# Eight small products in a row in front of a slot, in a kernel of attention and two layers

## The chip, the cores and the metric

The kernel runs on one core of a Trainium2 chip. The metric is the device time of one execution in microseconds, the median of several runs. TensorE (PE in the profile) multiplies, VectorE (DVE), ScalarE (ACT) and GpSimd (POOL) work on elements, and SyncE (SP) issues the DMAs.

## What is computed

Nystrom attention (4 batches, 8 heads, 576 tokens, head size 64, 32 landmarks), then two feed-forward layers of 2304 tokens, 512 wide, 2048 inside:

```python
q_lm = q.reshape(B, H, m, S // m, D).mean(axis=3)      # m = 32 landmarks
k_lm = k.reshape(B, H, m, S // m, D).mean(axis=3)
A, Bm, C = sm(q, k_lm), sm(q_lm, k_lm), sm(q_lm, k)    # softmaxes
Z = Bm.transpose(0, 1, 3, 2) / (norms of Bm)
for _ in range(6):
    Z = 2 * Z - Z @ Bm @ Z
x = A @ Z @ C @ v                                      # then heads side by side
h = x @ w_in;  x = (h * clip(h + 3, 0, 6) / 6) @ w_out
h = x @ w_in2; out = where(h > 0, h, exp(min(h, 0)) - 1) @ w_out2
```

## The kernel before

The attention is never multiplied out. For each batch a Newton stage (`newton`: landmarks, softmaxes, the inverse in six steps, and `finish`) makes a small matrix `mt` from Z, C and v. N = `mt` times the first layer's input weights takes the place of those weights, so that the first layer's h is A times N. N is made in four **parts** of 512 columns (`attn_n(b, c)`, line 764): for each of four 32-row blocks j and two head groups g one **product**, 64 deep, 32 wide, 512 columns, so eight products in a part. They write two PSUM banks of the pool "bk", which has two. ScalarE then copies each bank to `nh`, and VectorE subtracts to get the rest `nl` (a number is kept as a high and a low half). The input weights of a part come by DMA into the tile `w1c`, of which there are two, so that the part c + 2 can be loaded (`load_w1`, four DMAs on SP) when the part c has read its own.

The main work runs in **slots** (loop at line 1117). A batch has 32 slots: two halves of its tokens by 16 blocks of 128 inner units. `slot_a1` (line 791) makes h with six matmuls from `nh`, `nl` and the attention halves `ath`, `atl`; then ScalarE (relu into `gf`), VectorE, ScalarE (`gh`) and GpSimd (`gl`) make the activation. `slot_a2` (line 821), three slots later, adds the block to four outputs x with twelve matmuls from `gh`, `gl` and the weights. The h tile has two buffers. Part c of N is read by slots 4c to 4c + 3 of the first half, and again in the second half.

Beside the slots the planner places the Newton stage of the next batch, the parts of N (before: in slots 20, 24 and 28 of the batch before, and in slot 0 for the last part), and every third slot a conversion of later weights (`conv_out2`, `conv_in2`: a load, work on ScalarE, VectorE and GpSimd, a store).

The order on each engine is fixed when the program is built. Each step gets a due time (`wanted`, in slots), and a planner with its own model of durations puts the instructions of each engine in order. Two things bind it: data dependencies, and orders written by hand with `after` (line 117), which only say that one instruction is to be planned behind another. On one engine such an order costs no wait. All matmuls of the attention, `amm`, hang in one chain (`last`); the matmuls of the slots are free against them. `marks["slot"]` is the last matmul of the newest `slot_a1`.

Of the kernel before, what the change touches and what calls it, by code (L numbers as in the profile page):

```python
# [31 lines left out]
def nystrom_ffn_kernel(ctx: ExitStack, tc, q, k, v, w_in1, w_out1, w_in2, w_out2, out):  # L32
# [32 lines left out]
    B, G, _, _, S = q.shape  # L65
# [9 lines left out]
    NKT = DFF // 128  # L75
# [8 lines left out]
    MPC = W // 128  # L84
# [10 lines left out]
    GATE1, O2, NEW1 = 8, 3, 0  # L95
    PACE, NEW, PACE1 = 0.5, -4, 0.2
    XSET, XPACE = 4, 1

    strict = [False]

# [16 lines left out]
    def after(inst, other):  # L117

        tc.add_manual_dep(
            inst.ins, other.name, mybir.DependencyInfo(mybir.DependencyClass.NoSync, mybir.DependencyReason.DATA)  # L120
        )
# [4 lines left out]
    def sub(o, a, b, eng=vec):  # L126
        return eng.tensor_tensor(out=o, in0=a, in1=b, op=ALU.subtract)
# [18 lines left out]
    def mm(o, w, x, start, stop):  # L146
        return pe.matmul(o, lhsT=w, rhs=x, start=start, stop=stop)

    def wanted(s):
        tc.cur_priority = int(1000 * (s + 100))  # L150

    last = [None]

    def ordered(inst):

        if last[0] is not None:
            after(inst, last[0])
        last[0] = inst.ins
# [7 lines left out]
    def amm(*a):  # L166
        ordered(mm(*a))

    def atr(*a):
        ordered(pe.transpose(*a))  # L170

    x1d = dram.tile([NDM, 128, NT], F32, name="x1d")
    w1d = dram.tile([NDM, 128, DFF], F32, name="w1d")
# [5 lines left out]
    banks, marks = {}, {}  # L179

    def bank():
        return banks["att"].tile([128, 512], F32, name="bk", tag="bk")
# [48 lines left out]
    def run(gen):  # L231
        for _ in gen:
            pass
# [176 lines left out]
    def load_w1(b, c):  # L410
        t = w1_t[b, c] = w1_tile()
        for i in range(MPC):
            o = c * W + i * 128
            sp.dma_start(out=t[:, i], in_=w1d[:, :, o:o + 128].rearrange("k p n -> p k n"))
# [277 lines left out]
    def start():  # L692
# [15 lines left out]
        def fill(eng):  # L708
# [7 lines left out]

        make = {
            "k": preps, "f": lambda: finish(0, kept["Q"], cvs, sc), "n": lambda: attn_n(0, 0, 128),
            "i": lambda: keep("Q", inverse(EB, sb)), "t": lambda: attn_at(0, 0, vec),
        }  # L720
# [25 lines left out]
    def span(b, hf):  # L746

        n = T1 if b == 0 else HALF
        return (0, n) if hf == 0 else (n, S - n)

    def attn_at(b, hf, eng=pool):

        s, n = span(b, hf)
        ath = nat.tile([128, G, n], F32R, name="ath", tag=f"ath{hf}")
        atl = nat.tile([128, G, n], F32R, name="atl", tag=f"atl{hf}")
        for g in range(G):
            at = ft.tile([128, T2], F32, name="at", tag="at" if g or b or hf else "gf", bufs=1 if g or b or hf else 2)[:, 0:n]
            vec.transpose(out=at, in_=e_t[b, g][:, s // 32:(s + n) // 32, :].rearrange("p t l -> p (t l)"))
            yield
            act.copy(out=ath[:, g, :], in_=at)  # L760
            sub(atl[:, g, :], at, ath[:, g, :].bitcast(F32), eng)
        at_t[b, hf] = (ath, atl)

    def attn_n(b, c, n=W):

        nh = nat.tile([128, G, W], F32R, name=f"nh{c}", tag=f"nh{c}")
        nl = nat.tile([128, G, W], F32R, name=f"nl{c}", tag=f"nl{c}")
        n_t[b, c] = (nh, nl)
        w1 = w1_t[b, c]
        mt = mt_t[b]  # L770
        for o in range(0, W, n):

            nps = [bank()[:, 0:n] for _ in range(G)]
            for j in range(4):
                for g in range(G):
                    p0 = 64 * g
                    amm(nps[g][32 * j:32 * j + 32, :], mt[p0:p0 + 64, j, :],
                        w1[p0:p0 + 64, o // 128:(o + n) // 128, j, :], True, True)
            for g in range(G):
                h, l = nh[:, g, o:o + n], nl[:, g, o:o + n]  # L780
                act.copy(out=h, in_=nps[g])
                sub(l, nps[g], h.bitcast(F32))
            yield
        nb, nc_ = (b, c + 2) if c + 2 < NW else (b + 1, c + 2 - NW)
        if 0 < nb < B:
            load_w1(nb, nc_)
# [4 lines left out]
    def slot_a1(i):  # L791
        b, hf, m = i // SB, i // NKT % 2, i % NKT
        nt = span(b, hf)[1]
        ps = banks["h"].tile([128, 512], F32, name="h", tag="h")[:, 0:nt]
        c, o = m // MPC, m % MPC * 128
        nh, nl = n_t[b, c]
        ath, atl = at_t[b, hf]
        n = 0
        for g in range(G):
            for w, x in ((nh, atl), (nl, ath), (nh, ath)):  # L800
                marks["slot"] = mm(ps, w[:, g, o:o + 128], x[:, g, :], n == 0, n == 3 * G - 1).ins
                n += 1
        gf = ft.tile([128, T2], F32, name="gf", tag="gf", bufs=2)[:, 0:nt]
        yield
        act.activation(out=gf, in_=ps, func=AF.Relu, scale=1.0 / 6.0, bias=half_b)
        yield
        if i < NKT:
            g = gp.tile([128, T2], F32, name="g", tag="gh")[:, 0:nt]
            vec.scalar_tensor_tensor(out=g, in0=gf, scalar=1.0, in1=ps, op0=ALU.min, op1=ALU.mult)
            gt[i] = g, None  # L810
            return
        gh = gp.tile([128, T2], F32R, name="gh", tag="gh")[:, 0:nt]
        gl = gp.tile([128, T2], F32R, name="gl", tag="gl")[:, 0:nt]
        vec.scalar_tensor_tensor(out=gf, in0=gf, scalar=1.0, in1=ps, op0=ALU.min, op1=ALU.mult)
        yield
        act.copy(out=gh, in_=gf)
        yield
        sub(gl, gf, gh.bitcast(F32), vec if i >= NA - SB + XSET else pool)
        gt[i] = (gh, gl)

    def slot_a2(i, mm=mm):
        b, hf, kk = i // SB, i // NKT % 2, i % NKT
        gh, gl = gt.pop(i)
        s, nt = span(b, hf)
        for dm in range(NDM):
            if kk == 0:
                acc[dm] = banks["x"].tile([128, 512], F32, name="x", tag="x")[:, 0:nt]
            sl = slice(dm * 128, (dm + 1) * 128)
            if i < NKT:
                mm(acc[dm], wo[kk][:, sl], gh, kk == 0, kk == NKT - 1)  # L830
            else:
                wh, wl = wo[kk]
                for j, (w, x) in enumerate(((wh, gh), (wh, gl), (wl, gh))):
                    mm(acc[dm], w[:, sl], x, kk == 0 and j == 0, kk == NKT - 1 and j == 2)
            if kk == NKT - 1:
                t0 = b * S + s
                xs = ft.tile([128, nt], F32, name="xs", tag="xs", bufs=NDM)
                act.copy(out=xs, in_=acc[dm])
                sp.dma_start(out=x1d[dm, :, t0:t0 + nt], in_=xs)
            yield  # L840
# [205 lines left out]
    def second_half(slots):  # L1046
# [7 lines left out]
        def parts():  # L1054
            for c in range(NW):
                yield from attn_n(1, c, 256)
# [60 lines left out]
    for i in range(END, NA):  # L1117
        b, r = i // SB, i % SB

        wanted(i)  # L1120
        if r == 0:
            run(attn_n(b, NW - 1))
            run(attn_at(b, 1))
            if b + 1 < B:
                newton(b + 1)
            else:
                att.close()
                win.append(ctx.enter_context(tc.tile_pool(name="win", bufs=1, side="right", reuse_waits="tile")))
                xp.append(win[0])
                x0 = load_x(0, vec)  # L1130
        if b + 1 < B and r == NKT:
            run(attn_at(b + 1, 0))
        if b + 1 < B and r > NKT and r % MPC == 0:
            run(attn_n(b + 1, (r - NKT) // MPC - 1))
        if (i - END) % O2 == 0 and conv:
            gate[0] = marks["slot"]
            wanted(i + 4)
            conv.pop(0)()
            gate[0] = None
        if i >= NA - SB + XSET:  # L1140
            wanted(i + 4)
            next(x0, None)
        if i == NA - 14:
            wanted(i + 2)
            load_in2(0)
        wanted(i)
        run(slot_a1(i))
        run(slot_a2(i - DELAY))

    def late():  # L1150

        for i in range(NA - DELAY, NA):
            a2 = slot_a2(i, bmm)
            for _ in range(NDM):
                next(a2)
                yield
            run(a2)

    def seconds():
        for q in range(NTT * NQ):  # L1160
            yield from second(q)
# [3 lines left out]
    behind, tail, xs, n = seconds(), late(), x0, 0  # L1165
# [59 lines left out]
```

## Time and profile before

| | |
|---|---|
| median of 3 runs | 870.97 us (870.86 to 872.89) |
| the profiled execution | 872.62 us |
| its span | 870.8 us |
| granted clock, mean | 0.976 of 2.4 GHz |
| PE busy | 824.6 us (95%) |
| DVE, ACT, POOL busy | 519.2, 450.9, 321.9 us |

The time of the profiled execution is its span and 1.8 us around it. Matmuls overlap, so PE is counted busy from the first start to the last end; a busy PE may still do little. One product of fp32 numbers shows as two records. All engine instructions go through one helper, so every row names line 109, and instructions are told apart by their tiles: h and x are the slots' matmuls, bk those of the attention, "bk<-w1c,mt" the products of N.

### The profile page before, as it was taken

The numbers are of one execution on the slowest core, as the hardware profiler recorded it, in microseconds if no ns is written. First come the engines' busy times: TensorE is split into PE (matmuls) and PEld (weight loads), VectorE is DVE, ScalarE is ACT, GpSimd is POOL, SyncE is SP. The second block draws the span as 40 slices with busy tenths as digits, with TensorE's granted clock in tenths as the row PEclk, the third lists the DMA queues.
The fourth block names the chain that finished last, engine by engine and source line by source line (L and its number), as shares of the span: only waits on it lengthen the run. The fifth ranks groups of instructions, "written<-read, shape, count | busy, mean of one in ns | idle before, by whom it ended". The sixth has DMA issues, their size and how long they took to land.

```text
span 870.8 us, 15636 instructions
## 1 busy us (share of the span) xinstructions
PE 824.6 (95%) x5746; PEld 704.2 (81%) x5746; DVE 519.2 (60%) x1054; ACT 450.9 (52%) x1008; POOL 321.9 (37%) x330
## 2 busy tenths in 40 slices
PE   4778899999999999999999799999999999999998
PEld 3656678778985789858989699998989889999996
DVE  5579857647542465326688787775566554654544
ACT  2368645555553556537566565655454443443433
POOL 2257656636543445432244794551083000000000
PEclk9759999999999999999999899999999999999999
DMA  9377942285454532535366647677846556565441
GB/s 323 119 266 244 347 147 75 87 259 191 148 156 148 159 120 102 160 108 181 126 240 246 197 174 276 249 269 260 285 167 209 180 174 234 197 217 182 163 152 73
DMA packets 95564, 165.65 MB, mean 190 GB/s; under 512 B 7232, under 2 KB 51264, under 8 KB 95488
## 3 DMA queue, kind: packets, MB, share of 16 engines
q1 hardware_dynamic: 95488, 164.66, 55.8%
q8 instruction: 45, 0.74, 0.4%
q14 instruction: 31, 0.25, 0.1%
HBM read 119.54 MB, written 45.09 MB: 189 GB/s over the span
## 4 chain that ended last, share of the span: by engine, by line
PE 74%; DVE 7%; DMA 5%; POOL 4%; ACT 2%; issue 2%; SPq 0%; DVEq 0%; POOLq 0%; ACTq 0%
PE x L109 39%; PE h L109 28%; PE bk L109 7%; DVE h L109 1%; DMA kt<-in_k 1%; POOL x L109 1%; DMA out<-ob 1%; POOL xf L109 1%; DMA x<-x1d 1%; DVE w1c L109 1%; DVE y L109 1%; DVE gf L109 1%; DMA u<-in_moe_w_in 1%; DMA w1c<-w1d 1%; SPq L109 0%
## 5 line engine op out<-in xcount | busy, mean ns | idle before, releaser
L109 PE MATMUL h<-x,wi 128*128 128x384 f32 x1008 | 207.7, 341 | 6.4 <-DVE u L109 2.0
L109 PE MATMUL x<-gh,wo 128*128 128x288 f32 x896 | 204.3, 301 | 0.3 <-DVE wo L109 0.3
L109 PEld LDWEIGHTS h<-x,wi 128*128 128x128 f32 x1008 | 182.8, 190 | 21.8 <-DVE u L109 3.2
L109 PEld LDWEIGHTS x<-gh,wo 128*128 128x128 f32 x896 | 150.6, 188 | 18.2 <-issue 12.9
L109 PE MATMUL x<-gl,wo 128*128 128x288 f32 x448 | 131.8, 296 | 1.3 <-DVE gl L109 1.3
L109 ACT CAST gh<-gf 128x288 fp32r<-128x288 f32 (+1 forms) x172 | 79.1, 460 | 83.0 <-DVE gf L109 82.5
L109 PE MATMUL x<-w,gh 128*128 128x512 f32 x360 | 116.2, 393 | 0.0
L109 POOL TENSOR_TENSOR gl<-gf,gh 128x288 fp32r<-128x288 f32 x84 | 69.6, 830 | 98.7 <-ACT gh L109 88.9
L109 ACT ACTIVATE gf<-y 128x384 f32<-128x384 f32 x96 | 50.4, 525 | 98.7 <-DVE y L109 98.5
L109 DVE SCALAR_TENSOR_TENSOR gf<-gf,y 128x384 f32<-128x384 f32 x96 | 64.5, 672 | 59.0 <-ACT gf L109 59.0
L109 ACT ACTIVATE gf<-h,half_b 128x288 f32<-128x288 f32 x128 | 63.7, 500 | 62.0 <-PE h L109 52.2
L109 PE MATMUL h<-atl,nh 128*128 128x288 f32 x256 | 81.6, 319 | 9.9 <-DVE g L109 8.5
L109 DVE SCALAR_TENSOR_TENSOR gf<-gf,h 128x288 f32<-128x288 f32 x112 | 50.0, 448 | 66.9 <-ACT gf L109 66.2
L109 PE MATMUL x<-w,ghl 128*128 128x512 f32 x324 | 89.1, 392 | 0.0
L109 PEld LDWEIGHTS x<-gl,wo 128*128 128x128 f32 x448 | 84.4, 188 | 2.9 <-DVE gl L109 1.9
L109 PE MATMUL h<-ath,nh 128*128 128x288 f32 x256 | 77.9, 304 | 0.0
L109 PE MATMUL h<-ath,nl 128*128 128x288 f32 x256 | 77.8, 304 | 0.0
L109 PEld LDWEIGHTS x<-w,gh 128*128 128x128 f32 x360 | 67.4, 189 | 9.1
L109 PE MATMUL x<-w,gl 128*128 128x512 f32 x180 | 70.7, 393 | 0.0
L109 DVE TENSOR_TENSOR gl<-gf,gh 128x384 fp32r<-128x384 f32 (+1 forms) x88 | 57.6, 658 | 19.6 <-ACT gh L109 15.0
L109 PEld LDWEIGHTS h<-atl,nh 128*128 128x128 f32 x256 | 49.2, 192 | 22.7 <-DVE g L109 12.7
L109 PEld LDWEIGHTS x<-w,ghl 128*128 128x128 f32 x324 | 60.2, 188 | 8.4
(147 smaller groups left out, 1304.6 us busy)
## 6 DMA issues: line engine op xcount, KB each, us to landing
wi<-wi2p SPq DMA_DIRECT2D x64, 448.0 KB, 5.0
w<-wo2p SPq DMA_DIRECT2D x32, 512.0 KB, 6.0
wi2p<-wi SPq DMA_DIRECT2D x32, 448.0 KB, 2.7
u<-in_moe_w_in SPq DMA_DIRECT2D x25, 512.0 KB, 4.5
w1c<-w1d SPq DMA_DIRECT2D x48, 256.0 KB, 4.5
ub<-in_moe_w_out SPq DMA_DIRECT2D x16, 512.0 KB, 6.2
u<-in_moe_w_out SPq DMA_DIRECT2D x16, 512.0 KB, 4.3
wo2p<-w SPq DMA_DIRECT2D x16, 512.0 KB, 3.0
```

The costliest lines, as they stand in the source:

```text
L109: inst = getattr(self.eng, name)(*a, **kw)
```

## The change

In the third and fourth batch (b of 2 and 3) the first product of a part is ordered behind the last matmul of the slot before, of `slot_a1` (`marks["slot"]`) and of `slot_a2` (`prev[0]`), and all later matmuls of slots are ordered behind the part's last product (`hold`). The function `smm` stands in the place of `mm` in the slots for that. The parts 0 to 2 move to slots 25, 28 and 31 of the batch before; part 3 stays in slot 0.

```diff
     XSET, XPACE = 4, 1
+    NAT = 25, 28, 31
...
+    hold, prev = [None], [None]
+
+    def smm(*a):
+
+        inst = mm(*a)
+        if hold[0] is not None:
+            after(inst, hold[0])
+        prev[0] = inst.ins
+        return inst
...
             for j in range(4):
                 for g in range(G):
                     p0 = 64 * g
-                    amm(nps[g][32 * j:32 * j + 32, :], mt[p0:p0 + 64, j, :],
-                        w1[p0:p0 + 64, o // 128:(o + n) // 128, j, :], True, True)
+                    inst = mm(nps[g][32 * j:32 * j + 32, :], mt[p0:p0 + 64, j, :],
+                              w1[p0:p0 + 64, o // 128:(o + n) // 128, j, :], True, True)
+                    ordered(inst)
+                    if b > 1 and g == j == 0:
+                        after(inst, marks["slot"])
+                        after(inst, prev[0])
+            if b > 1:
+                hold[0] = last[0]
...
-                marks["slot"] = mm(ps, w[:, g, o:o + 128], x[:, g, :], n == 0, n == 3 * G - 1).ins
+                marks["slot"] = smm(ps, w[:, g, o:o + 128], x[:, g, :], n == 0, n == 3 * G - 1).ins
...
-    def slot_a2(i, mm=mm):
+    def slot_a2(i, mm=smm):
...
-        if b + 1 < B and r > NKT and r % MPC == 0:
-            run(attn_n(b + 1, (r - NKT) // MPC - 1))
+        if b + 1 < B and r in NAT:
+            run(attn_n(b + 1, NAT.index(r)))
```

## Rows read from the trace of the kernel before

**Rows 1.** The page, part 1: busy us of each engine (share of the span), instructions.

```profile
PE 824.6 (95%) x5746; PEld 704.2 (81%) x5746; DVE 519.2 (60%) x1054; ACT 450.9 (52%) x1008; POOL 321.9 (37%) x330
```

**Rows 2.** Stages: us, busy us (instructions) of each engine, granted clock, DMA share, GB/s.

```profile
247.00:286.00 39.00, 39.00 (x228) 24.12 (x227) 13.03 (x26) 17.19 (x38) 15.39 (x17) 1.00 0.54 163
...
357.00:396.00 39.00, 39.00 (x219) 23.18 (x218) 11.63 (x23) 15.54 (x33) 13.66 (x15) 1.00 0.50 158
```

**Rows 3.** Chain of waits in order of time, third batch's parts: start, us, what, instructions.

```profile
247.92 1.08 PE bk L109 x16
249.00 0.59 PE x L109 x3
...
251.97 0.80 PE h L109 x6
...
254.72 1.01 PE bk L109 x14
...
261.64 0.97 PE bk L109 x2
262.62 0.33 PE h L109
...
268.15 0.98 PE bk L109 x6
...
270.91 0.80 PE h L109 x6
271.71 1.58 PE x L109 x12
```

**Rows 4.** The same chain in the stretch of the fourth batch's parts.

```profile
358.00 1.02 PE bk L109 x16
359.02 1.52 PE x L109 x10
...
364.73 1.01 PE bk L109 x14
...
394.36 0.98 PE bk L109 x4
```

**Rows 5.** Timeline of VectorE: start, us, instruction, idle before and releaser.

```profile
250.58 1.29 DVE L109 TENSOR_TENSOR nl<-bk,nh 128x512 fp32r<-128x512 f32 x2 [0.98 <-ACT nh L109]
...
257.78 1.29 DVE L109 TENSOR_TENSOR nl<-bk,nh 128x512 fp32r<-128x512 f32 x2 [0.98 <-ACT nh L109]
...
269.80 1.29 DVE L109 TENSOR_TENSOR nl<-bk,nh 128x512 fp32r<-128x512 f32 x2 [0.48 <-ACT nh L109]
```

**Rows 6.** Timeline of SP's DMA issues, and the landing times of w1c, 246 to 290.

```profile
258.06 2.81 SPq L109 DMA_DIRECT2D w1c<-w1d  x4
...
359.15 8.72 SPq L109 DMA_DIRECT2D w1c<-w1d  x8
...
DMA to landing us min/median/max: 2.8/4.5/5.5
```

**Rows 7.** Timeline of VectorE: the copies that make mt.

```profile
247.57 0.28 DVE L109 COPY mt<-bk 128x128 f32<-128x128 f32 x1
...
355.59 0.28 DVE L109 COPY mt<-bk 128x128 f32<-128x128 f32 x1
```

**Rows 8.** Waits, 190 to 400 us: who on whom, us, times, longest.

```profile
PE bk L109 <- ACT EC L109: 0.4, 1, 0.4
...
ACT y L109 <- DMA u<-in_moe_w_out: 22.0, 9, 5.6
```

**Rows 9.** The page, part 5: busy us and mean ns of one, idle before.

```profile
L109 ACT ACTIVATE gf<-h,half_b 128x288 f32<-128x288 f32 x128 | 63.7, 500 | 62.0 <-PE h L109 52.2
...
L109 DVE SCALAR_TENSOR_TENSOR gf<-gf,h 128x288 f32<-128x288 f32 x112 | 50.0, 448 | 66.9 <-ACT gf L109 66.2
```

**Rows 10.** Chain of waits, 288 to 356 us: two of the Newton stage's pieces.

```profile
308.07 1.05 PE bk L109 x52
...
340.57 0.36 PE bk L109 x16
```

## The prediction

> **What bounds the kernel now.** I read the page first: TensorE (PE) is busy for 824.6 of the 870.8 us of the span [rows 1], so the question is what PE does in the stretches that the change touches. The stage table answers that: the two stretches in which the parts of N for the third and fourth batch are made, 247 to 286 us and 357 to 396 us, have PE busy throughout at a granted clock of 1.00 (the 2.4 GHz level), while VectorE, ScalarE and GpSimd work 12 to 17 us of 39 [rows 2]. PE's own wait list from 190 to 400 us holds one wait of 0.4 us, and that one lies outside both stretches [rows 8]. So PE sets the pace, and busy doesn't mean well used: the chain of waits, in order of time, shows what it is busy with.
>
> A slot without anything beside it is six matmuls into h (0.80 us) and twelve into x (1.58 us): 18 matmuls in 2.38 us, 0.132 us each [rows 3]. A part of N is eight products, sixteen records, 64 rows deep and 32 columns wide, so eight of them sit in the array side by side. Sixteen records in a row take 1.02 to 1.08 us on the chain; a piece of two records takes 0.97 us [rows 3, 4]. A piece costs what its longest member costs, whatever stands in it. The one slot matmul behind a piece then stands at 0.33 us instead of 0.13 [rows 3]. So a piece of two costs 0.97 + 0.20 = 1.17 us, a whole part 1.02 + (1.52 - 10 x 0.132) = 1.22 us in the fourth batch and 1.08 + 0.19 = 1.27 us in the third (three slot matmuls behind it took 0.59 us for 0.40).
>
> Counted on the chain, the parts of the third batch stand in 1, 2, 6 and 6 pieces, those of the fourth in 1, 2, 6 and 7: 31 pieces for 8 parts. Rows 3 and 4 show the whole parts, the long piece of each second part, and first and last of chopped ones; the others repeat them. From the third part on the planner puts one h matmul of a slot between every two records.
>
> **What the change does to that.** The ordering edges: the first product of a part goes behind the last matmul of the slot before (`marks["slot"]`, `prev[0]`), and every later slot matmul goes behind the part's eighth product (`hold`). All of these are orders on PE's own queue, so they add no instruction and no semaphore. The chain `last` already ties the products to each other and to Newton's matmuls, so nothing is left that could come between. I take 8 rows for 31 pieces.
>
> The parts also move, from slots 20, 24 and 28 of a batch to 25, 28 and 31 (the fourth stays at slot 0 of the next). With each go two ScalarE copies, two VectorE subtractions and four w1c loads on SP, past the store and load of one or two weight conversions, which come every third slot. GpSimd gets and loses nothing.
>
> The sum by stage: 39.00 us hold 228 matmuls in the third batch's stretch, 64 of them products and two reaching in from before; 162 x 0.132 = 21.4 us, so the parts cost 17.6 us. In the fourth, 219 - 66 = 153, 20.2 us, parts 18.8 us [rows 2]. Together 36.4 us, 1.17 for each of 31 pieces, which is the price read off the chain. Eight whole rows at 1.22 to 1.27 are 9.8 to 10.2 us; I take 10.0. **Gross gain 26.4 us**, all on PE, the engine that sets the end. Whatever follows is PE's too, so it moves forward whole.
>
> What was hidden in those 36 us and isn't any longer. A row in front of a slot holds the whole slot back if one of its inputs is late; in pieces, it held back little.
>
> - *mt.* Slots are counted back from the fourth part, which is planned with slot 0. In the trace the first part ran late anyway, in front of slot 24 in one batch and within it in the other, since mt came only then: its copy ends at 247.85 and 355.87 us [rows 7]. Slot 25's first matmul stands at 251.97 and at 359.02 + 1.52 = 360.54 us [rows 3, 4]; less the part that ran before it, 250.7 and 359.3. Spare 2.8 and 3.4 us: cost 0.
> - *The banks.* A part needs both banks of its pool, so row four (slot 0 of the next batch) waits for the copies of row three, one slot before. Between them lie 2.38 + 0.2 = 2.6 us. From the end of a part to the end of the second VectorE subtraction took 250.58 + 1.29 - 249.00 = 2.9 us, 3.3 us (from 255.73) and, where ScalarE was at it at once, 271.09 - 269.13 = 2.0 us [rows 3, 5]. Late by -0.6 to +0.7 us: cost 0 to 1.4 us for two batches. I take 0.8, nearer to the two late rows, as these stood behind whole rows.
> - *w1c.* The load that row four needs starts when row two has read its tile. After the second part the four issues began 2.3 us later and took 2.8 us; the slowest landed 5.5 us after its issue: 10.6 us at worst. In the fourth batch the issues ended 2.1 us after the part; with 4.5 us in the median, 6.6 [rows 4, 6]. Between row two and row four lie four slots and row three, 9.5 + 1.2 + 0.2 = 10.9 us: cost 0, bound 2 us if the queue stands behind a store. No queue gets an entry more.
> - *ScalarE's order.* Its queue also holds the conversions of later weights; it stood idle for their loads 9 times, 22.0 us, longest 5.6 [rows 8]. Part of that was covered, since PE was stretched by pieces. A slot's h bank is wanted two slots on: 4.76 - 0.80 - (0.50 + 0.45) = 3.0 us of spare behind its matmuls [rows 3, 9]. So a wait of 5.6 us right behind a row costs up to 2.6 us; the waits of the trace cost PE nothing. Four rows have a conversion beside them: 0 to 10 us. I take 1.0, near the rows at hand, since PE lost nothing even behind the whole rows.
>
> Net 26.4 - 0.8 - 1.0 = **24.6 us**. The profiled execution took 872.62 us (span 870.8, 1.8 around it), so it comes to 848.0; it lies 1.65 above the median of 870.97, which gives **846.4 us**. With nothing lost it is 844.3 to 844.8.
>
> **The rivals.**
>
> *B, new waits eat a good part.* Against it: no wait of PE in either stretch, and engines beside it that work 30 to 44% of it; with 13 us less in each stretch they come to 45 to 66%. For it: the planner orders ScalarE and VectorE by its own durations, and the two copies of rows three and four fall into neighbouring slots. Banks 1.4, w1c 2 and three full hold-ups of ScalarE 8: 11.4 us, so 15 gained: 856 us, with anything from 849.5 on. The Trainium skill speaks for this one (TensorEngine Tiling, Performance Considerations): packing small matmuls speeds up TensorE but not the evacuation of PSUM, which may become the bottleneck. By that rule alone row four waits in both batches, 1.4 us, and the time is 847.0; the trace agrees in that a row takes 1.0 us and its copies 2.0 to 3.3, but there it never made PE wait.
>
> *C, it does not do what it says.* If the pieces stayed and only slots moved: 871 us. Against: the two orders close the row from both sides.
>
> *D, slower.* The planner plans anew, and chops Newton's products of the fourth batch as it chopped the parts. They have no row of their own to stand in; today they run in pieces of 2 to 52 records, 21 between 288 and 356 us [rows 10]. A piece of 16 takes 0.36 us and some 0.2 behind it, so each cut adds about 0.5 us; 53 cuts beyond today's give back all of 26.4 us. A batch has 139 such products, so 100 cuts would lose 24 us: 895 us. Against it: their order isn't touched, and the pieces stand as they are beside the same slots.
>
> **How the numbers follow.** Forecast (all but a few us of the gain, 843.5 to 849.5) 0.75; better than that, by a plan that falls out luckily, 0.03; B 0.16; C 0.02; D 0.04. The range is the forecast's with the near half of B, 843.5 to 852. About 0.3%, 2.6 us, is what a measurement of this kernel can tell: faster 0.94, same 0.02, slower 0.04.
>
> **What would show it.** On the chain of the changed kernel: eight pieces of sixteen records each for the two batches, in front of slots 25, 28, 31 and 0, at 1.0 to 1.1 us; slots of 2.38 us between. The stretches of 39 us shrink to about 26. An idle PE in front of the fourth row, released by VectorE's subtraction, is the banks; one released by a DMA is w1c; an idle PE in front of an h matmul with ScalarE behind a load is the conversions. I am wrong if a row costs more than 1.3 us, if the pieces are more than eight, or if Newton's pieces between the stretches become more than some 25.

## The result, and the profile after

The changed kernel takes **851.95 us** in the median (851.1 to 852.09) beside 871.93 us of the kernel before (870.86 to 873.29; four executions, one more than above): a ratio of 0.9768, 95% interval 0.9749 to 0.9787. That is 20 us less; the prediction had said 846.4, in a range from 843.5 to 852. So the gain is real and of the kind that was forecast, and some 4 to 5 us of it went missing on the way; the time lies inside the range by 0.05 us only. The rest of this document is about where these went. Two executions far from all others, one of 985.56 us of the run with layer two's casts moved and one of 2737.63 us of the kernel before, were slow ones and are left out of every comparison.

The page of the changed kernel, part 1, answers [rows 1] (busy us of each engine, share of the span of 850.3 us):

```profile
PE 798.6 (94%) x5746; PEld 700.0 (82%) x5746; DVE 515.2 (61%) x1054; ACT 450.5 (53%) x1008; POOL 321.2 (38%) x330
```

PE does the same 5746 instructions in 26.0 us less, and that is the forecast gross gain of 26.4. But the span shrank by 20.5 only: the idle time of PE grew from 870.8 - 824.6 = 46.2 to 51.7 us. The pieces themselves stand in PE's timeline; its columns are start, us, instruction, and in brackets the idle time before it and who ended it. All eight rows of products of the third and fourth batch:

```profile
248.37 1.09 PE L110 MATMUL bk<-w1c,mt 64*32 64x512 f32 x16
256.71 1.09 PE L110 MATMUL bk<-w1c,mt 64*32 64x512 f32 x16
265.04 1.09 PE L110 MATMUL bk<-w1c,mt 64*32 64x512 f32 x16
269.36 1.68 PE L110 MATMUL bk<-w1c,mt 64*32 64x512 f32 x16 [0.67 <-DVE nl L110]
...
345.80 1.09 PE L110 MATMUL bk<-w1c,mt 64*32 64x512 f32 x16
354.13 1.09 PE L110 MATMUL bk<-w1c,mt 64*32 64x512 f32 x16
362.48 1.09 PE L110 MATMUL bk<-w1c,mt 64*32 64x512 f32 x16
366.07 1.09 PE L110 MATMUL bk<-w1c,mt 64*32 64x512 f32 x16
```

Eight pieces in the place of 31 [rows 3, 4], each of sixteen records. One of the eight is late: the last of the third batch waits 0.67 us for VectorE's subtraction, and is 0.59 us longer in itself, since VectorE was done with its second bank only at 269.91 us, 0.55 after the row had begun. On the chain of waits (start, us, what) a row and its slot now read

```profile
362.55 1.02 PE bk L110 x16
363.57 1.00 PE h L110 x6
364.57 1.58 PE x L110 x12
366.14 1.02 PE bk L110 x16
367.16 0.98 PE h L110 x6
```

The first h group behind a row takes 0.98 to 1.00 us where a free one takes 0.80: the 0.2 us behind a piece. PE's waits from 190 to 400 us, which [rows 8] showed as one of 0.4 us (columns: who waits for whom, us, times, longest):

```profile
PE x L110 <- ACT xs L110: 2.0, 2, 1.8
PE bk L110 <- DVE nl L110: 0.7, 1, 0.7
PE h L110 <- DVE gf L110: 0.4, 1, 0.4
PE bk L110 <- ACT EC L110: 0.3, 1, 0.3
PE bk L110 <- ACT ect L110: 0.2, 1, 0.2
```

To see where the time went I cut both executions at four places that are the same in each program: the first matmul from Qd (the end of the third batch's Newton stage), the same one in the fourth batch, the first h matmul of layer two, and the first x matmul of layer two's second kind (x<-w,gh; the stretch before it is called the **seam** below). For each stretch its length, and PE's busy time:

| stretch | before: us, busy | after: us, busy | less time | less busy | more idle |
|---|---|---|---|---|---|
| start to first Qd | 244.39, 211.25 | 242.14, 210.13 | 2.25 | 1.12 | -1.13 |
| Qd to Qd (third batch's parts) | 109.41, 109.41 | 98.21, 97.33 | 11.20 | 12.08 | 0.88 |
| Qd to h (fourth batch's parts) | 119.95, 117.70 | 108.80, 104.06 | 11.15 | 13.64 | 2.49 |
| seam, h to x | 24.94 | 28.34 | -3.40 | | |
| x to the end | 372.11 | 372.81 | -0.70 | | |

The program up to the first Qd is the same in both, so the first row is spread between executions, not gain. The two stretches of the parts gave 22.35 us, where 24.6 was forecast; the seam, which the change doesn't touch, took 3.4 back.

In front of the first x of layer two's second kind stand nine groups of six h matmuls. The end of the seam in the timeline of PE, of before and then of after: the ninth group, and for after also the seventh and eighth, which are merged in one line.

```profile
496.61 2.29 PE L109 MATMUL h<-x,wi 128*128 128x384 f32 x6 [1.82 <-ACT a L109]
498.69 1.05 PE L109 MATMUL x<-w,gh 128*128 128x512 f32 x2
```

```profile
466.45 4.64 PE L110 MATMUL h<-x,wi 128*128 128x384 f32 x12 [2.62 <-DVE u L110]
475.41 2.29 PE L110 MATMUL h<-x,wi 128*128 128x384 f32 x6 [4.32 <-DVE y L110]
477.49 1.05 PE L110 MATMUL x<-w,gh 128*128 128x512 f32 x2
```

The last group before the first x waited 1.8 us for ScalarE's copy `a` in before and waits 4.3 us for VectorE in after, and the two groups ahead of it run at half speed (granted clock 0.50 from 466 to 478 us, the 1.2 GHz level; six matmuls take 2.3 us and not 1.3). PE's own order of instructions is the same here in both kernels. What differs is ScalarE's: in before the copy `a<-h` stood ahead of a cast of `wi` and one of `gh`, in after behind them.

```profile
496.08 0.47 ACT L109 COPY a<-h 128x384 f32<-128x384 f32 x1
496.45 0.62 ACT L109 CAST wi<-u 128x512 fp32r<-128x512 f32 x1
496.98 0.51 ACT L109 CAST gh<-gf 128x384 fp32r<-128x384 f32 x1
```

```profile
472.45 0.62 ACT L110 CAST wi<-u 128x512 fp32r<-128x512 f32 x1
472.98 0.51 ACT L110 CAST gh<-gf 128x384 fp32r<-128x384 f32 x1
473.39 0.47 ACT L110 COPY a<-h 128x384 f32<-128x384 f32 x1
```

That copy frees an h bank; since it is late, the two h banks change places, and the ninth group waits for the reader of the other bank, which is VectorE.

The two waits for `xs` (ScalarE's copies that free the x accumulators) have their cause in ScalarE's timeline:

```profile
279.54 0.67 ACT L110 ACTIVATE y<-u 128x512 f32<-128x512 f32 x1 [3.18 <-DMA u<-in_moe_w_out]
...
281.06 0.98 ACT L110 COPY xs<-x 128x288 f32<-128x288 f32 x3
...
374.98 0.51 ACT L110 CAST x<-x 128x384 fp32r<-128x384 f32 x1 [1.60 <-DMA x<-x1d]
375.80 0.51 ACT L110 CAST x<-x 128x384 fp32r<-128x384 f32 x1 [0.31 <-DMA x<-x1d]
...
376.61 0.99 ACT L110 COPY xs<-x 128x288 f32<-128x288 f32 x3
```

ScalarE stands idle at an instruction whose load has not landed, and the copies that PE wants are queued behind it. The first of the two loads is a conversion's, and cost PE 0.2 us; the second, 1.8 us, is of layer two's x (x1d). The late row has the first cause:

```profile
266.55 0.67 ACT L110 ACTIVATE y<-u 128x512 f32<-128x512 f32 x1 [2.15 <-DMA u<-in_moe_w_out]
...
268.00 1.06 ACT L110 CAST nh<-bk 128x512 fp32r<-128x512 f32 x2
```

The bank copies `nh` could have begun at 266.1, when row three had ended; the stop lasted until 266.55, two instructions of the conversion and a cast of `gh` followed, and the copies began at 268.00; VectorE's subtractions came right behind, at 268.62, and the row at 269.36.

### The profile page after: what moved, and what is told of

Its sections match the earlier page's. It is cut to its first block, busy times and chain, and to the rows that moved or that the text cites. A ratio compares the mean times of both kernels' runs of the same rounds, so it can differ in the third digit from the quotient of the medians.

```text
span 850.3 us, 15640 instructions
## 1 busy us (share of the span) xinstructions
PE 798.6 (94%) x5746; PEld 700.0 (82%) x5746; DVE 515.2 (61%) x1054; ACT 450.5 (53%) x1008; POOL 321.2 (38%) x330
## 4 chain that ended last, share of the span: by engine, by line
PE 71%; DVE 8%; DMA 6%; POOL 3%; issue 3%; ACT 3%; SPq 0%; POOLq 0%; DVEq 0%; ACTq 0%
PE x L110 39%; PE h L110 27%; PE bk L110 5%; DVE h L110 1%; POOL x L110 1%; DMA wi2d<-y 1%; DVE y L110 1%; DMA out<-ob 1%; POOL xf L110 1%; DVE gf L110 1%; DVE u L110 1%; DVE w1c L110 1%; DMA wo2d<-y 1%; DVE nl L110 1%; DMA u<-in_moe_w_out 1%
## 5 line engine op out<-in xcount | busy, mean ns | idle before, releaser
L110 PE MATMUL x<-gh,wo 128*128 128x288 f32 x896 | 201.9, 299 | 2.3 <-ACT xs L110 2.0
```

What stands on the lines that cost most here:

```text
L110: inst = getattr(self.eng, name)(*a, **kw)
```

## The experiments

Each kernel is the changed one with the edit shown, unless it says otherwise; "stages" are the stretches of the table above.

### What a piece costs

**The slots moved, no orders.** The products stand in slots 25, 28 and 31, and the planner may put slot matmuls between them.

```diff
-                    if b > 1 and g == j == 0:
-                        after(inst, marks["slot"])
-                        after(inst, prev[0])
-            if b > 1:
-                hold[0] = last[0]
```

> The parts in slots 25, 28 and 31, without the orders: the planner then leaves the eight parts in 41 pieces (31 in the kernel before, 8 in the changed one). Theory P (the gain is the number of pieces at 1.17 us): 10 pieces more than before, 11.7 us, about 883 us, give or take a seam of 3 us. Rival (the gain comes from the later place, at which mt and the loads are ready): 855 to 868 us.

Measured: 881.33 us, ratio 1.0104 (1.0074 to 1.0133), **slower than before**. The planner cuts the parts into 41 pieces, ten more than before: in the third batch the first three parts stand in six pieces each, where before only the third and fourth did. The second part in PE's timeline:

```profile
263.52 1.04 PE L110 MATMUL bk<-w1c,mt 64*32 64x512 f32 x2
...
270.03 1.06 PE L110 MATMUL bk<-w1c,mt 64*32 64x512 f32 x6
```

The two stages are 12.2 us longer than before, 1.22 for each of the ten pieces, against 1.17 in the prediction's sum. The place alone gives nothing; what counts is the number of pieces.

**Six rows cut in two.** Parts 0 to 2 of both batches run four products in front of the slot, then the slot's first h matmul, then the other four: 14 pieces.

```diff
+                    if b > 1 and g == 0 and j == 2 and c < 3:
+                        after(inst, marks["slot"])
+                if b > 1 and j == 1 and c < 3:
+                    hold[0] = last[0]
+                    yield
...
```

> The changed kernel with six of the eight rows cut in two, four products, one h matmul of the slot, four products: 14 pieces for 8. Theory P (a piece costs 0.97 us and 0.20 behind it whatever stands in it): six pieces more at 1.17, 7.0 us more, about 859 us; 3.4 less if the seam comes back to the old plan by itself, about 855.5. Rival (what costs is the number of products between full matmuls, not the number of pieces): no more than 1 us.

Measured: 857.29 us, ratio 0.9834 (0.981 to 0.9858). A half of eight records takes 1.06 us, a whole row of sixteen 1.09. The stages are 4.7 and 4.2 us longer than after the change, for three more pieces in each (3.5 by the price of 1.17). Of the 8.9 us 8.0 are busy time of PE, 1.33 for each of the six pieces, and 0.9 idle time. So the number of pieces is what counts, at a price somewhat above the one read off before. The seam came out at 24.74 us, though nothing near it was edited.

### What the two halves of the change do

**Orders without the move**: `NAT = 20, 24, 28`.

> The orders, with the parts in their old slots 20, 24 and 28: eight whole rows, but the first of a batch stands in front of slot 20, some 4 slots before the Newton stage had mt ready in the kernel before. Theory W (a row in front of a slot stops TensorE until mt is there, and Newton's chain of small steps runs on alone): the pieces give 26 us, two stops take 4 to 9 us each, about 855 to 866 us, with the idle TensorE in front of the first row. Rival (the planner fits the Newton stage in front, since its due times are earlier): 846 to 852 us.

Measured: 863.34 us, ratio 0.9895 (0.9868 to 0.9921). PE's timeline in front of the first rows:

```profile
241.70 0.47 PE L110 MATMUL bk<-Qd,t 128*64 128x128 f32 x4 [1.53 <-DVE Qd L110]
242.55 1.96 PE L110 MATMUL bk<-w1c,mt 64*32 64x512 f32 x16 [0.38 <-DVE mt L110]
...
342.90 0.44 PE L110 MATMUL bk<-Qd,t 128*64 128x128 f32 x4 [1.83 <-DVE Qd L110]
343.72 1.40 PE L110 MATMUL bk<-w1c,mt 64*32 64x512 f32 x16 [0.38 <-DVE mt L110]
```

With the rows in the old slots the end of Newton's chain is drawn in front of them, and PE, which has to keep the row in a piece, stands and waits for it: from 230 to 242 us it is busy 8.83 us of 12 and from 330 to 345 us 12.17 of 15, where in before it was busy throughout. The first rows take 1.96 and 1.40 us, at a granted clock of 0.79 over the 8 us that begin there. So more than half of the 20 us is lost if the rows are not moved to where `mt` is ready; the move is worth some 11 us with the orders and less than nothing without.

**One batch only**, first the third, then the fourth (`b == 2` or `b == 3` in the place of `b > 1`, with the old slots for the other batch).

> Rows and new slots in the third batch only, the fourth as in the kernel before; the seam has the copy first, as in the kernel before. Theory P: 15 pieces become 4, 12.6 us off, less 1.3 us of bank wait: about 860.5 us. Rival (most of the measured gain belongs to the fourth batch): above 864.

> Rows and new slots in the fourth batch only; the seam has the copy first, as in the kernel before. Theory P with the seam's theory S: 16 pieces become 4, 13.8 us off, less up to 2.2 us of waiting for the accumulators' copies, no loss at the seam: 858 to 860.5 us. If the seam is long whenever the fourth batch is faster (rival to S): 862 to 864.

Measured: 863.2 us, ratio 0.9874 (0.9827 to 0.9921), and 862.61 us, ratio 0.9888 (0.9861 to 0.9914). Alone the third batch's stage is 12.0 us shorter than before, the fourth's 10.5. By the ratios the two gains are 1.26% and 1.12%, 2.4% together, beside 2.3% for both at once: each batch pays for itself. Both times are longer than expected (860.5, and 858 to 860.5), and the second lies where its rival had put it; but the seam stayed at 25.8 and 24.7 us, so the rival's reason, that the faster stage of the fourth batch makes the seam long, is not what happened.

### Where the missing microseconds went

**The seam's copy ahead of the casts.** ScalarE's copy `a<-h` gets the place in ScalarE's order that it had in before.

```diff
...
-        act.copy(out=a1, in_=block(0, 0))
+        inst = act.copy(out=a1, in_=block(0, 0))
+        if q == 1:
+            after(marks["wi", 2, 0], inst.ins)
+            after(marks[0, 1, 0], inst.ins)
```

> The changed kernel with one ScalarE copy moved: at the seam of the two layers, the copy that frees an h bank of the second quartet goes ahead of two casts that the new plan had put before it, as in the kernel before; nothing else is moved on any engine, and the third group of h matmuls at the seam then waits for ScalarE instead of VectorE. Theory S (3.4 us of the expected gain were lost at the seam, because the new plan swapped the two h banks there): about 848.5 us, 3.4 less than the 851.95 of the changed kernel, and the stretch from the first h matmul of layer two to its first x matmul is back from 28.3 to about 25 us. Rival (the seam is longer because TensorE's clock fell earlier or the DMAs of wi came late, and the bank is only what the wait is put down to): within 1 us of 851.95.

Measured: 851.55 us, ratio 0.9757 (0.9736 to 0.9778). In the seam it does what was expected, as PE's timeline shows:

```profile
470.63 2.07 PE L110 MATMUL h<-x,wi 128*128 128x384 f32 x6 [1.05 <-DVE y L110]
473.63 2.29 PE L110 MATMUL h<-x,wi 128*128 128x384 f32 x6 [0.93 <-ACT a L110]
```

The wait of 4.3 us is gone, the seam takes 24.73 us and not 28.34. The clock did fall earlier in after, as the rival had it (the seventh group runs at half speed there and takes 1.3 us here), but that isn't what makes the seam long: the eighth group ends 21.9 us after the seam's start there and 21.7 us here, and the difference comes behind it. The median fell by 0.4 us only, which is where the rival had put it. Of the 3.6 us in the traces 1.5 were lost elsewhere: the span counted from the first Qd is 606.0 us beside 608.2. So the mechanism is shown in its stretch; what it is worth in the median can't be told apart from nothing (the two intervals overlap almost entirely).

**The third row one slot earlier**: `NAT = 25, 28, 30`, so that two slots lie between rows three and four.

> The changed kernel with the third part in front of slot 30 instead of 31, so that two slots lie between rows three and four. Theory K (row four of the third batch waited 0.67 us in front and some 0.6 us inside for the copies of row three): 1.2 to 1.3 us less, 850.7, and the row behind slot 32 takes 1.09 us in the timeline instead of 1.68 with no idle before it. Rival (the wait is passed on to another place, as ScalarE still waits for the conversion's load): within 0.5 us of 851.95.

Measured: 850.29 us, ratio 0.976 (0.9736 to 0.9784), with executions from 848.28 to 854.53: the median is near the expected 850.7, but its interval covers most of that of the changed kernel, so the median decides nothing. The trace, of the longest execution, does. Row four stands in PE's timeline without a wait, and 13 us later there is this:

```profile
270.57 1.09 PE L110 MATMUL bk<-w1c,mt 64*32 64x512 f32 x16
...
283.09 0.40 PE L110 MATMUL x<-gh,wo 128*128 128x288 f32 x1 [1.20 <-ACT xs L110]
```

The 1.26 us of the bank are gone, 1.2 us of waiting for `xs` have come (0.2 there in after), and the stage is shorter by 0.27 us. In this trace the wait was passed on to the next instruction that ScalarE is late with: the bank was where it showed, not its cause.

**The casts of layer two's x behind the accumulators' copies.** The first casts that wait for x1d are ordered behind `xs` on ScalarE.

```diff
...
+        if behind is not None:
+            after(inst, behind)
...
-                act.copy(out=xs, in_=acc[dm])
+                marks["xs"] = act.copy(out=xs, in_=acc[dm]).ins
...
```

> The changed kernel with the casts of the first x tiles of layer two ordered on ScalarE behind the copies of the accumulators at the end of the half before. Theory A (the 1.79 us that TensorE waits for the accumulators' copies at slot 99 come from ScalarE standing in front of a cast whose load had not landed): 1.8 to 2.2 us less if the seam stays as it is, 850.0, and no wait of x matmuls for those copies there; the casts come later, so the seam may move by itself. Rival (the copies are late for another reason): the wait stays, within 0.5 us of 851.95.

Measured: 851.0 us, ratio 0.9759 (0.9735 to 0.9782), no gain that can be told from nothing. From the first Qd to layer two the waits for `xs` fell from 2.0 to 1.2 us, 0.6 at the longest, but PE waits 1.3 us for `gl` (0.2 in after) and 0.4 for `gh` in their place, and is idle for 6.6 us beside 5.6; the planner moved other work, ScalarE's stops at the conversions' loads (`in_moe_w_out` and `in_moe_w_in`) among them, which make up 19.8 us in that stretch, beside 11.3 in after. An order that is meant for one wait changes the plan around it.

**The conversions' work two slots behind their load.** If the common cause is that ScalarE stands at a cast whose load has not landed, then all of those waits should go at once when the cast is planned later. The load is issued as before; the casts and the store come two slots later, each behind a matmul of that slot.

```diff
+    LATE = 2
...
+        gen = steps(part(w_out2, kk, 0), room(), y)
+        next(gen)
...
-            conv.pop(0)()
+            rests.append(conv.pop(0)())
+            gate[0] = None
+        if (i - END) % O2 == LATE and rests:
+            gate[0] = marks["slot"]
+            wanted(i + 4 - LATE)
+            rests.pop(0)()
...
```

> The changed kernel with each weight conversion of the slots cut in two: the load as before, the work on ScalarE, VectorE and GpSimd planned two slots later, behind a slot matmul of that time. Theory A (the waits of TensorE for the accumulators' copies, for the banks of row four and for gf come from ScalarE standing in front of a conversion whose load takes 4.5 to 6.4 us to land): these waits go, some 3.5 us less between the Newton stages of the two batches and the seam, 848.5 us, and ScalarE's list of waits has less than 8 us on those loads between 240 and 450 us. Rival (the copies are late whatever stands in front of them): the waits stay, 851 to 853 us.

Measured: **843.06 us**, ratio 0.9671 (0.9645 to 0.9698), 8.9 us less than the changed kernel. PE's waits from the first Qd to layer two, 5.6 us of idle time in after, are now

```profile
PE h L111 <- DMA wi2d<-y: 1.3, 1, 1.3
PE x L111 <- DVE gl L111: 0.6, 1, 0.6
PE x L111 <- ACT gh L111: 0.4, 1, 0.4
```

and ScalarE's own, for loads of the conversions, 4.6 us in the place of 11.3:

```profile
ACT y L111 <- DMA u<-in_moe_w_in: 2.8, 3, 2.2
...
ACT y L111 <- DMA u<-in_moe_w_out: 1.8, 1, 1.8
```

No wait for `xs`, `nl` or `gf` is left in the stretches of the parts, and the rows stand at 1.09 us, row four of the third batch too. From row to row, from the first of the third batch to the first of the fourth, it is 95.80 us beside 97.43: the 1.63 are the 1.26 of the bank, the 0.2 of `xs` and little else. In all PE is busy 797.4 us (798.6 in after) and idle 43.7 (51.7): 8.0 of the 9.2 us between the two spans are idle time. 3.4 of those 8.0 us lie between the first Qd and layer two, where the expectation had put it; 3.3 lie behind the start of layer two, the seam's among them, and 1.3 ahead of the first Qd. From the third batch's first row to layer two, the same 1672 matmul records in both, it is 196.4 us beside 200.8: 4.4 us are gained in the stretch that the expectation was about, and it had said 3.5. But not all of that is the conversions' own: the 1.8 us of `xs` in the fourth batch stood behind casts of layer two's x, which this edit doesn't touch. In this trace ScalarE doesn't stop for x1d at all from the fourth batch's Qd to layer two, and runs the four `xs` copies at 370.70 to 372.79 us; whether the new order of ScalarE or an earlier landing of the loads does that was not tested.

**The same, one slot behind**: `LATE = 1`.

> The same cut with one slot between load and work; this plan has the h banks of the seam as the kernel before had them. Theory A with theory S: some 1.5 us less by the waits and 3.5 at the seam, 847 us. Rival: 851 us.

Measured: 848.34 us, ratio 0.9716 (0.9691 to 0.974): between the two. ScalarE's waits for the conversions' loads are 14.4 us here, not fewer than in after, and PE still waits 0.9 us for `nl` and 2.0 for `gf`, but no longer for `xs`; the seam came out at 24.73. So the sum of ScalarE's stops doesn't decide, only what is queued behind each.

**The kernel before, traced again**, to see what two executions of one program differ by.

> The kernel before, traced once more. If the last layer from its first x matmul to the end takes 374 to 375 us here as in the runs with one batch changed, those 2 to 3 us are the spread between executions; if it takes 372 again, a layer that begins earlier really gives 2 us back.

Measured: 871.88 us. From the first x of layer two's second kind to the end it took 374.03 us, 1.9 more than the first time; up to the first Qd 241.63, 2.8 less. So a difference of 2 to 3 us in one of these two stretches between two traces says nothing on a change.

**The kernel before, with the conversions two slots behind their load**: are those 9 us to be had without the rows?

> The kernel before, in pieces and without orders, with the work of a conversion on ScalarE, VectorE and GpSimd two slots behind its load, as in the run that did the same to the changed kernel. Theory A (ScalarE's stops at the loads cost time only where rows have taken the cover away): ScalarE's waits for the loads fall as they did there, from 23.0 us between the first Newton stage's end and layer two to some 5, and TensorE gains nothing by it before layer two, since it waited for ScalarE not once in the parts' stretches: stages of 109.5 and 119.8 us stay within 1.5 us each; the median stays within 0.3% of the kernel before, 869 to 875 us, but for a new plan in the seam of the layers (24.9 us, which may move by 5 either way). Rival (the later place of the conversions is worth the same 9 us to any kernel): about 863 us, with the two stages 3 to 5 us shorter together.

Measured: 865.8 us, ratio 0.9944 (0.9921 to 0.9966): neither the 869 to 875 of the one nor the 863 of the other. ScalarE's waits for the conversions' loads are gone (0.3 us left of 23.0). PE had not waited beside the parts; at the end of the last batch it had waited 2.0 us for `gf` and 0.2 for `gl`, and waits 0.2 and 0.8 now, so 1.2 us of idle time are gone. Yet from the first Qd to layer two it takes 8.4 us less. With the conversions two slots later the first Qd stands eight matmuls later in PE's order, 1.06 us at 0.132 each, so 7.4 us are left for the same work. The parts stand there in 26 pieces, not 31; the fourth batch's third part in PE's timeline, which takes three pieces now and took six:

```profile
367.19 1.07 PE L110 MATMUL bk<-w1c,mt 64*32 64x512 f32 x10
369.04 1.04 PE L110 MATMUL bk<-w1c,mt 64*32 64x512 f32 x2
370.34 1.05 PE L110 MATMUL bk<-w1c,mt 64*32 64x512 f32 x4
```

Five pieces at 1.17 us are 5.9 of the 7.4 us, and the idle time is most of the rest. The median fell by 5.8. My expectation had left out that the planner, given other work, also cuts the parts in other places. In the changed kernel it can't: there the pieces are eight with the conversions early or late, and PE's busy time differed by 1.2 us.

Six of the kernels in one table: pieces of the parts, and the time from the first Qd to layer two. The two with the conversions two slots later have 1.06 us added for the eight matmuls that stand ahead of the first Qd there.

| kernel | pieces | us |
|---|---|---|
| slots moved, no orders | 41 | 241.5 |
| before | 31 | 229.4 |
| before, conversions later | 26 | 222.0 |
| rows cut in two | 14 | 215.9 |
| after | 8 | 207.0 |
| after, conversions two slots later | 8 | 202.6 |

Between before and the last line, both with 2.2 us of idle time of PE in these stretches, lie 26.7 us for 23 pieces, 1.16 each.

## Why the prediction was right, and where it was off

The direction, the mechanism and the gross gain were right. The time lies in the stated range, but by 0.05 us, and outside the forecast's own band of 843.5 to 849.5: it is where rival B had its times, and the range reached that far only because it took in the near half of B.

**The price of a piece held.** 26.4 us gross were forecast; in the two stages PE is busy 12.08 + 13.64 = 25.7 us less, and the 0.6 us that the late row is longer in itself make 26.3. A row costs 1.09 us in the timeline and 0.2 behind it. The moved slots fit the same price (1.22), as does the difference between before and the last kernel of the table (1.16); the cut rows come to 1.33, and why they are dearer is open.

***mt* and w1c: cost 0, as forecast.** The first rows start 5.1 and 3.8 us after the end of the copy of `mt` (243.29 and 342.05 beside [rows 7]); no row waits for a DMA.

**The banks: 0.8 forecast, 1.26 measured,** within the 1.4 of the bound, but for another reason than the sum had, and all of it in one batch. The sum took the distance of two rows against the time of the copies, and so both batches would be late by the same. The fourth batch's row four didn't wait; the third's did, since ScalarE stood at a load and had the conversion's work ahead of the copies. That the size came out near is luck. The Trainium skill (TensorEngine Tiling (Array Packing), Performance Considerations) says that tiling doesn't speed up the evacuation of PSUM, whose copy may become the bottleneck. The trace agrees in one batch of the two, 1.26 us, and there the copies were late because they began 1.9 us after the row's end.

**ScalarE's order: 1.0 forecast, 2.0 and more measured.** The mechanism was the one named, a load with PE's work queued behind it, but 1.8 of the 2.0 us stood behind loads of layer two's x and not behind a conversion's. [Rows 8] gives only the stops at one of the two weights: the same view has three more, 6.2 us, at `in_moe_w_in`, so ScalarE stood 28.2 us and not 22.0. The place was wrong: I had worked out the spare of an h bank, and PE waited for the x accumulators' copies `xs`, twice, 2.0 us, and 0.7 more for `gf` at the end of the last batch. The idle time grew by 0.88 + 2.49 = 3.4 us in the two stages, with 0.67 of it the bank's, where the sum had 1.8 for all. My reason for the low value was that "the waits of the trace cost PE nothing". They cost nothing because pieces of 1.17 us stretched the slots beside them; that this cover goes was said, and not priced. The runs fit this, though none isolates it: in the third batch's stage ScalarE stood 15.5 us at the conversions' loads with 15 pieces and 17.4 us with 20, and PE was idle 0 and 0.2 us; with 4 rows 10.1 us went with 0.9.

**The step that failed** is "Whatever follows is PE's too, so it moves forward whole". Layer two's first h came at 449.15 us and not at 473.75, 24.6 us earlier (2.25 of it the start's spread). Then the seam lasted 3.4 us longer. The time behind the change is not a block that is pushed forward: the planner makes the whole order anew, and a copy on ScalarE two casts later in that order turned a wait of 1.8 us into one of 4.3. In five other kernels with rows the seam came to 24.7 to 25.8 us without an edit of that copy, in the one with row three earlier to 28.2, in the ones with layer two's casts moved and with the conversions two slots later to 17.4 and 19.1 (there the stretch behind it took 377.9 and 378.2 us, 5 us more than in after, so part of the time only moved past the landmark); and the edit of that one copy brings it back. So it hangs on how the plan falls out and isn't owed to the rows as such. What the prediction called "a plan that falls out luckily" it had with a chance of 0.03 on the good side, and on the bad side only in the form of Newton's products being cut; these stayed as they were (60 pieces beside 59). Of the rivals, B had the mechanism that showed, new waits, at 11.4 us where 3.4 came in the two stages and 3.4 more at the seam, a place that it didn't name.

The rest is the reference: I went from the profiled execution to the median by taking off 1.65 us, as before's profiled execution lay above its median by that. Beside the runs of after it lay 0.7 above before's median, and that of after lay 0.1 above its own. So of the 5.55 us between 846.4 and 851.95 about 1.5 are this, and 4.1 are in the span: 2.25 in the stages, 3.4 in the seam, 0.7 at the end, less 2.25 at the start.

**What stays open.** Why the edit of the seam shows 3.6 us in its stretch and 0.4 in the median; how much of the gain with the conversions two slots later comes from the conversions' loads and how much from a plan that fell out well, at the 1.8 us of `xs` and behind the start of layer two (3.9 of the 9.2 us), since that edit makes the order anew from 186 us on. One trace of each can't tell that, with 2 to 3 us of spread in the stretches next to it.

## What to carry over

Where matmuls of a small tile stand between large ones, count the pieces in which they run, not the products: here each costs 1.2 us whatever it holds, and the orders that close a piece pay only where its inputs are ready, or the engine stands in front of it. When the engine that sets the end gets faster, look at the queues beside it for an instruction that waits for a load with that engine's work behind it, and plan the use of a load later than its landing; the version that does so for the conversions is 8.9 us faster here, 4.4 of them in the stretch where the waits had been found (and part of these by a plan that fell out well), while three edits to single waits gave none that could be measured. And where a planner makes the order, no stretch behind the edit is sure to stay as it was: compare stage by stage, and give the seams a share in the range.

## What the runs showed of the hardware

The length of a piece in the timeline hardly depends on what is in it: 1.04 us for two records, 1.06 for eight and 1.09 for sixteen. I had read that from the trace before; the cut rows show it for the same products in both forms.

The clock followed PE's stops at two places where I hadn't looked for it. In the run with orders alone, PE was busy 8.83 of 12 us in front of the first row, and the granted clock over the next 8 us was 0.79; the row took 1.96 us. In the seam the columns of the stretches (us, busy us and instructions of PE, PEld, DVE, ACT, POOL, granted clock, DMA share, GB/s) show it in the changed kernel:

```profile
449.00:460.00 11.00, 8.44 (x49) 7.61 (x50) 9.60 (x12) 4.22 (x10) 11.00 (x10) 1.00 0.48 153
460.00:466.00 6.00, 3.83 (x25) 3.60 (x24) 3.47 (x6) 3.79 (x10) 4.86 (x5) 0.98 0.64 232
466.00:475.40 9.40, 4.58 (x12) 3.56 (x12) 7.38 (x15) 5.32 (x12) 3.87 (x5) 0.50 0.54 179
475.40:478.00 2.60, 2.59 (x8) 2.50 (x9) 1.96 (x4) 1.60 (x4) 2.32 (x3) 0.50 0.41 133
```

From 460 to 466 us PE was busy for 3.83 of 6 us, and a stop of 2.6 us began at 463.8; from 466 to 478 us the granted clock was 0.50: eighteen matmuls of h took 6.9 us, and 4.0 would have done at the 1.31 to 1.34 us of a group of six at full clock. In before the last group ahead of the first x took 2.29 us too, with a granted clock of 0.73 from 493.7 to 500 us.
